# Finding a row's 32 top scores on the maxima of column quadruples, pairs and single columns, under a new instruction order

## Chip, cores and metric

The kernel runs on one core of a Trainium2 chip. The metric is the device time of one execution in microseconds (us). A core has TensorE (PE), VectorE (DVE), ScalarE (ACT), GpSimd (POOL) and SyncE (SP, which here only issues transfers); each works through its own list of instructions in program order, and semaphores tie the lists together.

## What is computed

Three parts follow each other: sparse attention, a mixture of experts with one expert per token, and a SoLU block. For the change only the first matters. There are 4 batches, 8 heads, 576 positions and head size 64.

```
scores = scale * np.matmul(q, k.transpose(0, 1, 3, 2))          # [4, 8, 576, 576]
kth  = np.partition(scores, -32, axis=-1)[..., -32:-31]          # the row's 32nd largest
scores = np.where(scores >= kth, scores, -1e9)
attn = softmax(scores);  x = attn @ v                            # 2304 tokens of 512
x = moe(x)      # gate, argmax expert e, relu(x @ w1[e]) @ w2[e], scaled by the gate
x = solu_block(x)   # x @ w_in, h * softmax(h), layer norm, @ w_out
```

So each of the 18432 rows of 576 scores needs its 32nd largest value as a threshold.

## The kernel before

**Units.** The attention is cut into 144 units: a tile of query rows against all 576 keys of one head (for the last 64 rows of a batch, of two heads). A unit's scores lie in two PSUM banks of 288 columns each, `pS[0]` and `pS[1]` (L628); one block of matmuls fills the banks of two units. There are 8 PSUM banks in all, and every other matmul group of the kernel uses them too.

**A unit's steps (function `unit`).** ACT copies both banks to `ss` in SBUF (L649, L659). DVE writes into `W` the larger of columns c and c+288 (`M`, L661) and the smaller (`m`, L662); then the two banks are given back. On the 288 values of `M` DVE takes the eight largest three times (L665, and L672 twice), and each time strikes them out with a match-and-replace (L669, which the profile shows as a short value load and the pass itself). A last pass takes the eight largest of what is left in all 576 columns of `W` (L678); its eighth is the row's threshold. POOL turns the threshold into a bias (L689), ACT and POOL mask the scores (L690, L691), ACT takes the exponential (L693). The largest value, negated and scaled on POOL (L666), is the bias of the exponential.

**Is the threshold right?** It is, as long as no more than eight of the row's top 32 are hidden behind a larger partner. `flags` in `route` checks this for a tile's units with three small POOL operations (L810 to L812): the threshold must not be above the eighth value of the third round, kept in `abt`. Where a row breaks it, the end of the kernel runs the whole attention again in another way; with the inputs here this part isn't entered.

**After the units.** `pair` transposes the weights of two units (L722), multiplies with v (L755) and projects (L765). `route` finds each token's expert and scatters its row to a list in DRAM. When enough tokens are routed (`PLAN`: the first slot at 256 tokens), a block of 128 tokens of one expert is gathered and goes through the two expert layers (L1025, L1046) and the SoLU block (L1067, L1128). The last expert work after the last unit has its own matmuls (L1326, L1346). Beside the first units, `doubles` and the `static_` functions turn the float64 weights `w_in` and `w_out` into pairs of float32 (DVE L386, L388, L390; POOL L385, L394; PE L408).

**Order.** All of this is written as generators. `Order.run` takes the next step from one of the threads that are ready, and which one is written out digit by digit in the string `ORDER`: it fixes the order of the instructions on every engine. The costs in `Op(...)` are not used when the string is given.

Of the kernel before, what the change touches and what calls it, by code (L numbers as in the profile page):

```python
# [8 lines left out]
F32 = mybir.dt.float32  # L9
# [5 lines left out]
OP = mybir.AluOpType  # L15
# [24 lines left out]
    "0022556001101111220112334441144455551445446666556657427747773222333327775335888447777436655355541288886662"  # L40
    "2233223377544545420880112434236636663555662111122220111115455512445515551511211444454422222112223333666113"
    "3677784664844663352111111114453311466771167444662422235434533444363637777333312222234322221144466551518833"
    "4435355339777288224444113324677688511211211155334446665565666222372233333113333445655777771161168722024833"
    "364422764382847945557586992411222555222a4488333989442aa292277444a33335563351353366887025343333211555467771"
    "8331873333226226676888853113114444112222551114666566788437777221214222352111138335117133335562222688137331"
    "1122666223222222235112441111112255451611114334444444133111111666656a147372244aa3a3677774455556119427135517"
    "7761261369999787111173632227776224251111133888171113445356658591113713163122241322220112222243111364111555"
    "5111156776334777754544116666657333522253254343442133244452226222233441611554545451145762678742523411524162"
    "22222225514322324455555555133155404551451162351344434336201166666773113222204472226565568117772222027a6644"
    "2266464472211535668637322022222226234211516656511613540701811001175772221192999991335336676626241121334343"  # L50
    "3422555576337144457752056556777776215277441122834266512111342551133443434111111321155111222312444312444689"
    "aa2333029166334862388066005582200012aaa0777bb8998934541622627600052200011131722264677550113332300005665771"
    "1170031302720170043355600466411520041444300222668822888899999882484113267676788595956678666666925441122656"
    "5651777834222574441772263345689181074232222220673604122673357761573325887774644455712263522222222664541341"
    "1045414324420011144552254555514660021440013400000024234556745440055522115552561878733155684688777751336544"
    "5522223362222205541140343146455552226111731022557441213374221168484911556614642265506443433375366777121111"
    "533706773363254599899a689548155555524459476611342216655611177671835511677634226577117786311153888645222222"
    "7771222233662545456605571436222443151232342444666511500012000440000313112111343433671170010055667322114331"
    "1363465555221111455220630073322228265511576466723111112603666353357006664700007700729944477777833a66688289"
    "0116a1119187115166734448376675373887777333833a122456647838833266776765567837833468512131331225837225554312"  # L60
    "8011202544504355355302277788226646344878976772222222331099482615452333043334466610030778151121467633320077"
    "7000003700555555666111661615657776300662449983332347756264545456668999a3033745564541133688784444699aa84781"
    "032284813361447676111114611868841110100915546644444488129878a77899896b7579467a8877122553999aaa892258444708"
    "45444333333126634452122553347773116433316611142222885344366112995522833b4477366622211544112322285673558511"
    "63633737112288887452220221166555562278855073355536111711460111aaa452289a88582123aabb498999aa40330330244496"
    "98a64001988a5511614744832110155578828474643998754087785533446633633226233620666666462231777177220776267884"
    "4348446940178787878666666789785261511884412377779974664537725512274646464677447367776122451172444562222213"
    "1225568816667421477776565657112322146554253325466222246225776345520223257717554223777754662253345563333342"
    "08227851115111066114456608000077777211265627589aa0155a9966185556667493355689994533444744444588337798996998"
    "9851155767678885588894411941545584422333663336222111153353114113354553652834547778223455456331677727777565"  # L70
    "6333332333365646666778722224111551122442551771134552423112222222373773354445892288777722222238444b37757527"
    "ab77771115325aa5888892472231118378838808794946466522988328482414663899988881121442997265651165651133344116"
    "25777777786746966a45579aaaabb744668747454442554918847833367676035669999777a1255115344931111222228868296353"
    "6456464664377311855255511552222122111534347766266115653678722465657752222544666256533011449352448433326467"
    "451573334457577162222533112266885272433689aa89956555222267679222788887393312242222131816766333478877775650"
    "254477757875753aa788328807553a91455826333388036733305422224263315653368888365557247333357722222599889634b3"
    "999222558789bb000755877333333888377088255558366a43333994660019a9a80733440000030444335664438744337766777000"
    "0042211138885555116166111333510000220511666221454444161157703633333464111166666576335782446651621173633625"
    "5053446016577644449359a50446757776133336643346637332783311557544440066650074330000436626667722774665543442"
    "2503433847777455277131111115662255346424336225643377205677116614589777888262222277163111006667334665755462"  # L80
    "2131747511070656565114444434455657000045566667777aabaa4111111b478879666bb754832244305365655779247227733530"
    "3333266477122335575030007577362545588944000566500688874ba7822210033613331566555452222200882233662652454544"
    "7577586657838504727671466726665664412273422522277667782644324228816711455244522656756587644566733221322444"
    "3338331666244422275500044006666200000564177552285333083304822222255136651100115656008057366660000446500077"
    "67700667a7724117703442320005357745664465566633333331151116753305354334555667772292960002224667776664211123"
    "22535355360725522223222244388377644473322815656556255227777721222264675239225772886888700a7782255611646565"
    "7916111118170036786443344735833838383004444441142551400641255124542004104023232322134444124544113112216671"
    "5277666524466956557347767762211117111116423325560355356772235744370111627666888247866224533355224833308858"
    "8223446441114555711111714432211443337750411442362152335407733300000666000055001334133331113444102334444122"
    "2200122200111111100112321122110000010000022334402022330000000001122222334422440304444331152234000333366666"  # L90
    "6666663333316334755001553444444435000551172233366222010204331133333302222220000111002222322322320033300246"
    "6611100011101103345522100222311131231112233443311102001000332222333002000000000001000000000000002330002223"
    "3222222330223314334443221143333221122452400220110000000000303011112210003301101111111111112222201110021120"
    "1111110302211110022110100000"
# [145 lines left out]
def attn_moe_solu_kernel(ctx, tc, q, k, v, mid, w_gate, mbias, w1, w2, w_in, w_out, g_ln, out):  # L240
# [49 lines left out]
    flag = cst.tile([128, H], F32, name="flag")  # L290
# [347 lines left out]
    def unit(b, t, p, s, abt, tht, u, no, done):  # L638
# [22 lines left out]
        tM = yield Op("DVE", 369, lambda: nc.vector.tensor_tensor(M, pS[1], ss[:, :HALF], op=OP.max), deps=[t0])  # L661
# [1008 lines left out]
```

## Time and profile before

| | us |
|---|---|
| three runs | 943.79, 941.67, 943.60 (median 943.6) |
| the profiled execution, its own time | 944.39 |
| span of the profiled execution, first to last instruction | 942.5 |
| busy: PE / DVE / ACT / POOL | 874.3 / 773.9 / 670.3 / 582.4 |
| mean granted TensorE clock, as a share of 2.4 GHz | 0.967 |

The time is that of the whole execution; the span inside it is 1.9 us shorter. Busy times are of engines that work side by side, so they don't add up to the span. A DVE instruction's duration reaches past the start of the next one: durations overlap, and what an instruction costs a full queue is the distance from its start to the next start.

### The profile page before, as it was taken

The page shows a single profiled execution, that of the slowest core. Times are in us where ns is not written, and L with a number is a line of the kernel's source. Part 1 is how long each engine was busy: PE and PEld are TensorE (multiplying, and loading weights), DVE is VectorE, ACT ScalarE, POOL GpSimd, SP SyncE. Part 2 cuts the span into 40 slices and gives each one's busy share as a digit, 9 for nine tenths or more (in the row PEclk, how much of TensorE's full clock was granted, in tenths as well). Part 3 has the DMA queues.
Part 4 walks back from the last instruction along what each step waited for, and adds up shares of the span by engine and source line. Part 5 has one row for each costly group of instructions (what it writes and reads, how often), then busy time and mean ns, then how long its engine had stood idle before and what let it go on. Part 6 is the DMA issues. An engine that isn't in the chain of part 4 may idle for free.

```text
span 942.5 us, 21521 instructions
## 1 busy us (share of the span) xinstructions
PE 874.3 (93%) x6830; PEld 729.7 (77%) x6830; DVE 773.9 (82%) x2444; ACT 670.3 (71%) x1698; POOL 582.4 (62%) x1352
## 2 busy tenths in 40 slices
PE   5876787999999999999999999999999999999994
PEld 3443445987888888888878888788888988889883
DVE  7899989998999999999999999999999952432331
ACT  4777776879787778888877898788778872633432
POOL 4677866667657676676476767766776676531223
PEclk9878788999999999999999999999999999999998
DMA  6624323534623343464334434443432337723001
GB/s 157 196 68 128 103 91 92 146 106 125 192 80 122 119 140 99 128 160 140 104 90 122 142 93 135 146 119 113 129 100 84 112 107 210 235 79 112 24 12 37
DMA packets 140952, 110.72 MB, mean 117 GB/s; under 512 B 47233, under 2 KB 116893, under 8 KB 140830
## 3 DMA queue, kind: packets, MB, share of 16 engines
q1 hardware_dynamic: 136478, 93.92, 34.8%
q0 software_dynamic: 4352, 15.34, 4.8%
q8 instruction: 56, 0.92, 0.4%
q14 instruction: 66, 0.54, 0.2%
HBM read 97.11 MB, written 12.13 MB: 116 GB/s over the span
## 4 chain that ended last, share of the span: by engine, by line
PE 64%; DVE 11%; POOL 6%; ACT 5%; issue 3%; DMA 1%; POOLq 0%; DVEq 0%; ACTq 0%
PE ph L1025 10%; PE ph L1067 9%; PE py L1046 9%; PE po L1128 8%; PE po L755 6%; PE pS L628 5%; PE pt L722 5%; DVE M L669 2%; PE py L1346 2%; PE ph L1326 2%; POOL e L691 2%; PE px L765 2%; PE pt L960 2%; PE pw L408 2%; DVE tht L678 1%
## 5 line engine op out<-in xcount | busy, mean ns | idle before, releaser
L691 POOL TENSOR_TENSOR e<-ss,e 128x576 f32<-128x576 f32 x144 | 204.7, 1423 | 55.6 <-ACT e L690 54.1
L693 ACT ACTIVATE e<-e,nb 128x576 f32<-128x576 f32 x144 | 111.8, 777 | 22.8 <-POOL e L691 22.1
L669 DVE MATCH_REPLACE8 M<-tops,M 128x288 f32<-128x288 f32 x288 | 127.6, 446 | 0.0
L1025 PE MATMUL ph<-xT,wraw 128*128 128x128 f32 x960 | 126.9, 279 | 0.0
L1046 PE MATMUL py<-hh,wraw 128*128 128x128 f32 x960 | 125.8, 278 | 0.0
L690 ACT ACTIVATE e<-ss,bt 128x576 f32<-128x576 f32 x144 | 111.1, 776 | 14.6 <-POOL bt L689 14.3
L1025 PEld LDWEIGHTS ph<-xT,wraw 128*128 128x128 f32 x960 | 115.5, 191 | 6.0 <-issue 3.8
L1046 PEld LDWEIGHTS py<-hh,wraw 128*128 128x128 f32 x960 | 115.4, 192 | 4.2 <-issue 2.4
L1128 PE MATMUL po<-wo,lT 128*128 128x512 f32 x432 | 112.3, 405 | 0.5 <-DVE lT L968 0.2
L755 PE MATMUL po<-eT,vt 128*64 128x128 f32 (+1 forms) x1600 | 105.1, 273 | 7.5 <-ACT eT L725 3.3
L1067 PE MATMUL ph<-wi,yT 128*128 128x512 f32 x432 | 109.7, 402 | 0.0
L678 DVE MAX8 tht<-M 128x8 f32<-128x576 f32 x144 | 108.0, 753 | 0.9
L755 PEld LDWEIGHTS po<-eT,vt 128*64 128x64 f32 x1600 | 85.0, 140 | 24.1 <-ACT eT L725 6.9
L628 PE MATMUL pS<-kT,qT 64*128 64x288 f32 (+1 forms) x864 | 91.5, 324 | 3.9 <-DVE M L662 2.8
L725 ACT ACTIVATE eT<-pt 128x512 f32<-128x512 f32 x144 | 82.4, 598 | 15.7 <-PE pt L722 14.9
L1128 PEld LDWEIGHTS po<-wo,lT 128*128 128x128 f32 x432 | 77.5, 188 | 20.7 <-DVE lT L968 3.4
L1067 PEld LDWEIGHTS ph<-wi,yT 128*128 128x128 f32 x432 | 78.5, 188 | 18.2 <-issue 1.2
L722 PE MATMUL pt<-identr,e 128*128 128x128 f32 x576 | 84.2, 280 | 6.2 <-ACT e L693 3.3
L628 PEld LDWEIGHTS pS<-kT,qT 64*128 64x128 f32 (+1 forms) x864 | 71.6, 197 | 20.7 <-issue 8.8
L722 PEld LDWEIGHTS pt<-identr,e 128*128 128x128 f32 x576 | 67.2, 144 | 15.5 <-ACT e L693 4.3
L649 ACT ACTIVATE ss<-pS 128x288 f32<-128x288 f32 x144 | 58.0, 411 | 22.1 <-PE pS L628 15.1
L661 DVE TENSOR_TENSOR M<-pS,ss 128x288 f32<-128x288 f32 x144 | 64.9, 451 | 9.9 <-ACT ss L659 7.7
(256 smaller groups left out, 1826.1 us busy)
## 6 DMA issues: line engine op xcount, KB each, us to landing
wraw<-in_moe_w_dram SPq DMA_DIRECT2D x256, 256.0 KB
kr<-in_k_dram SPq DMA_DIRECT2D x32, 128.0 KB
qr<-in_q_dram SPq DMA_DIRECT2D x16, 256.0 KB
raw<-in_moe_w_out_dram SPq DMA_DIRECT2D x8, 512.0 KB
vt<-in_v_dram SPq DMA_DIRECT2D x32, 128.0 KB
raw<-in_moe_w_in_dram SPq DMA_DIRECT2D x8, 512.0 KB
wstage<-da SPq DMA_DIRECT2D x8, 256.0 KB
wc<-wstage SPq DMA_DIRECT2D x8, 256.0 KB
```

Of the source, the lines that this page charges most:

```text
L628: nc.tensor.matmul(bank[s][hf], x[r, a, p, :], kt[r, c, at:at + HALF], start=i == 0, stop=i == 2)
L669: nc.vector.match_replace(out=M, in_to_replace=rounds[r], in_values=M, imm_value=NEG)
L678: t0 = yield Op("DVE", 660, lambda: nc.vector.max(th, W), deps=[t0, tm])
L690: yield Op("ACT", 667, lambda: nc.scalar.activation(e, ss, AF.Relu, bias=bt, scale=-BIG))
L691: yield Op("POOL", 1360, lambda: nc.gpsimd.tensor_tensor(e, ss, e, op=OP.subtract))
L693: yield Op("ACT", 760, lambda: nc.scalar.activation(e, e, AF.Exp, bias=nb, scale=0.125, accum_out=z))
L722: nc.tensor.transpose(pt[:, c, :], ef[:, at:at + 128], ident)
L755: nc.tensor.matmul(po[hs, :n], w, x, start=c == 0, stop=c == 4)
L1025: nc.tensor.matmul(ph[:, :n], w[:, kk * 128:(kk + 1) * 128], x[0][:, kk, :n], start=kk == 0, stop=kk == KD - 1)
L1046: nc.tensor.matmul(py[c // k_][:, c % k_, :], w[:, c * 128:(c + 1) * 128], hs[m], start=m == 0 and c % k_ == 0, stop=m == KF - 1 and c % k ...
L1067: nc.tensor.matmul(ph, y[a][:, kk, :], wi[b][:, kk, i * 512:(i + 1) * 512], start=kk == 0 and j == 0, stop=kk == KD - 1 and j == 2)
L1128: nc.tensor.matmul(po, l[a][:, c, :], wo[b][:, kk, :], start=kk == 0 and j == 0, stop=kk == KF - 1 and j == 2)
```

## The change

`W` is used in four quarters. `Q` is the largest of four columns (c, c+144, c+288, c+432), 144 values; it is built from two maxima of 144 (one of them written to the first half of the bank `pS[0]`) and their maximum, and their minimum goes to `q`, beside it. `m`, the smaller of each pair, is made as before. Two rounds of eight now run on `Q` (144 values), the third on `M` = `Q` and `q` (288), the last on all 576. The two banks are given back after the five elementwise operations instead of after two. `abt` holds nine values per unit, so that the eighth of the second round stands beside the eighth of the third, and `flags` compares the threshold with both: its three POOL operations are twice as wide. `ORDER` is replaced as a whole.

```
 ORDER = (
...
-    flag = cst.tile([128, H], F32, name="flag")
+    flag = cst.tile([128, 2 * H], F32, name="flag")
...
-        M, m = W[:, :HALF], W[:, HALF:]
+        M, m, Q, q = W[:, :HALF], W[:, HALF:], W[:, :HALF // 2], W[:, HALF // 2:HALF]
         th = tht[:, u]
-        tops = sb.tile([128, 16], F32, tag="tops", name="tops", bufs=BUF["tops"])
-        rounds = [tops[:, 0:8], tops[:, 8:16], abt[:, u]]
+        tops = sb.tile([128, 8], F32, tag="tops", name="tops", bufs=BUF["tops"])
+        rounds = [(tops, Q), (abt[:, u, 1:9], Q), (abt[:, u, 0:8], M)]
...
-        tM = yield Op("DVE", 369, lambda: nc.vector.tensor_tensor(M, pS[1], ss[:, :HALF], op=OP.max), deps=[t0])
+        h, g = HALF // 2, pS[0][:, :HALF // 2]
+        ta = yield Op("DVE", 215, lambda: nc.vector.tensor_tensor(Q, pS[1][:, :h], ss[:, :h], op=OP.max), deps=[t0])
+        tb = yield Op("DVE", 215, lambda: nc.vector.tensor_tensor(g, pS[1][:, h:], ss[:, h:HALF], op=OP.max), deps=[t0])
         tm = yield Op("DVE", 369, lambda: nc.vector.tensor_tensor(m, pS[1], ss[:, :HALF], op=OP.min), deps=[t0])
+        tq = yield Op("DVE", 215, lambda: nc.vector.tensor_tensor(q, g, Q, op=OP.min), deps=[ta, tb])
+        t0 = yield Op("DVE", 215, lambda: nc.vector.tensor_tensor(Q, g, Q, op=OP.max), deps=[ta, tb])
         yield "put", ("B", 2)
-        t0 = tM
-        t0 = yield Op("DVE", 369, lambda: nc.vector.max(rounds[0], M), deps=[t0])
-        tn = yield Op("POOL", 179, lambda: nc.gpsimd.tensor_scalar(nb, tops[:, 0:1], -0.125, None, op0=OP.mult), deps=[t0])
-        for r in range(3):
-            def mr(r=r):
-                nc.vector.match_replace(out=M, in_to_replace=rounds[r], in_values=M, imm_value=NEG)
-
-            def mx(r=r):
-                nc.vector.max(rounds[r + 1], M)
-
-            t0 = yield Op("DVE", 369, mr, deps=[t0])
-            if r < 2:
-                t0 = yield Op("DVE", 369, mx, deps=[t0])
+        for r, (best, among) in enumerate(rounds):
+            t0 = yield Op("DVE", 216 if r < 2 else 369, lambda: nc.vector.max(best, among), deps=[t0, tq])
+            if r == 0:
+                yield Op("POOL", 179, lambda: nc.gpsimd.tensor_scalar(nb, tops[:, 0:1], -0.125, None, op0=OP.mult), deps=[t0])
+            t0 = yield Op("DVE", 272 if r < 2 else 420, lambda: nc.vector.match_replace(
+                out=among, in_to_replace=best, in_values=among, imm_value=NEG), deps=[t0])
...
-            f = small("fl", H, F32, 2)
-            nc.gpsimd.tensor_tensor(f[:, :nu], tht[:, :nu, 7], abt[:, :nu, 7], op=OP.subtract)
-            nc.gpsimd.tensor_scalar(f[:, :nu], f[:, :nu], 0.0, None, op0=OP.is_gt)
-            nc.gpsimd.tensor_tensor(flag[:, :nu], flag[:, :nu], f[:, :nu], op=OP.add)
+            f = small("fl", 2 * H, F32, 2).rearrange("p (u r) -> p u r", r=2)[:, :nu]
+            sofar = flag.rearrange("p (u r) -> p u r", r=2)[:, :nu]
+            nc.gpsimd.tensor_tensor(f, bc(tht[:, :nu, 7], 2, 2), abt[:, :nu, 7:9], op=OP.subtract)
+            nc.gpsimd.tensor_scalar(f, f, 0.0, None, op0=OP.is_gt)
+            nc.gpsimd.tensor_tensor(sofar, sofar, f, op=OP.add)
...
-                abt = sb.tile([128, H, 8], F32, tag="ab", name="abt", bufs=BUF["xs"])
+                abt = sb.tile([128, H, 9], F32, tag="ab", name="abt", bufs=BUF["xs"])
```

## Rows read from the trace of the kernel before

**Rows 1.** The page's list of engines: busy us, share of the span, instructions.

```profile
PE 874.3 (93%) x6830; PEld 729.7 (77%) x6830; DVE 773.9 (82%) x2444; ACT 670.3 (71%) x1698; POOL 582.4 (62%) x1352
```

**Rows 2.** Busy time by stretch: stretch, its length, each engine, PEclk, DMA.

```profile
25.00:160.00 135.00, 102.44 (x565) 62.35 (x563) 124.90 (x341) 99.04 (x231) 95.97 (x142) 0.82 0.36 109
160.00:770.00 610.00, 599.52 (x5254) 520.46 (x5255) 579.33 (x1907) 491.34 (x1285) 412.50 (x1016) 0.99 0.42 122
770.00:905.00 135.00, 133.94 (x858) 119.36 (x855) 42.65 (x126) 56.40 (x136) 51.33 (x137) 1.00 0.40 122
905.00:943.00 38.00, 24.66 (x113) 19.22 (x111) 9.01 (x19) 13.06 (x24) 11.21 (x28) 0.88 0.08 30
```

**Rows 3.** PE in order of time within 260 to 300 us.

```profile
275.85 1.95 PE L1046 MATMUL py<-hh,wraw 128*128 128x128 f32 x16
277.73 1.31 PE L755 MATMUL po<-eT,vt 128*64 128x128 f32 x20
```

**Rows 4.** L678 alone by stretch, as before (one per unit).

```profile
0.00:25.00 25.00, 1.42 (x2) 1.00 0.64 164
25.00:160.00 135.00, 15.05 (x20) 0.82 0.36 109
160.00:770.00 610.00, 91.52 (x122) 0.99 0.42 122
```

**Rows 5.** DVE's groups by line and shape: busy us, mean ns, idle before.

```profile
L669 DVE MATCH_REPLACE8 M<-tops,M 128x288 f32<-128x288 f32 x288 | 127.6, 446 | 0.0
L678 DVE MAX8 tht<-M 128x8 f32<-128x576 f32 x144 | 108.0, 753 | 0.9
L665 DVE MAX8 tops<-M 128x8 f32<-128x288 f32 x144 | 65.2, 453 | 0.0
L661 DVE TENSOR_TENSOR M<-pS,ss 128x288 f32<-128x288 f32 x144 | 64.9, 451 | 9.9 <-ACT ss L659 7.7
...
L669 DVE MATCH_VALUE_LOAD M<-tops,M 128x8 f32 x288 | 23.5, 82 | 0.7
...
L776 DVE TENSOR_TENSOR xs<-px,rz 128x144 f32<-128x144 f32 x16 | 4.8, 299 | 0.0
```

**Rows 6.** DVE in order of time, 305 to 310 us: start, duration, instruction.

```profile
305.75 0.45 DVE L662 TENSOR_TENSOR M<-pS,ss 128x288 f32<-128x288 f32 x1
306.12 0.45 DVE L665 MAX8 tops<-M 128x8 f32<-128x288 f32 x1
306.48 0.07 DVE L669 MATCH_VALUE_LOAD M<-tops,M 128x8 f32 x1
306.54 0.44 DVE L669 MATCH_REPLACE8 M<-tops,M 128x288 f32<-128x288 f32 x1
306.90 0.08 DVE L669 MATCH_VALUE_LOAD M<-tops,M 128x8 f32 x1
...
307.69 0.29 DVE L776 TENSOR_TENSOR xs<-px,rz 128x144 f32<-128x144 f32 x1
307.90 0.08 DVE L669 MATCH_VALUE_LOAD M<-abt,M 128x8 f32 x1
...
308.69 0.75 DVE L678 MAX8 tht<-M 128x8 f32<-128x576 f32 x1
309.35 0.08 DVE L669 MATCH_VALUE_LOAD M<-tops,M 128x8 f32 x1
```

**Rows 7.** DVE in order of time, 12 to 14 us, with few units in flight.

```profile
12.89 0.45 DVE L672 MAX8 tops<-M 128x8 f32<-128x288 f32 x1
13.37 0.09 DVE L669 MATCH_VALUE_LOAD M<-tops,M 128x8 f32 x1
```

**Rows 8.** PE's longest wait of 160 to 770 us: us, times, longest.

```profile
PE px L765 <- ACT e L690: 4.6, 1, 4.6
```

**Rows 9.** What PE waited for over the whole span, one row.

```profile
PE pS L628 <- DVE M L662: 2.8, 2, 2.6
```

**Rows 10.** POOL's flag operation at two widths.

```profile
L811 POOL TENSOR_SCALAR fl<-fl 128x8 f32<-128x8 f32 x16 | 4.2, 264 | 1.4
...
L811 POOL TENSOR_SCALAR fl<-fl 128x4 f32<-128x4 f32 x4 | 1.0, 250 | 0.4
```

More of the change, by code (lines that the diff above doesn't have):

```diff
@@ L45 @@
[L45 to L59, printed above, removed]
@@ L90 @@
[L90 to L94, printed above, removed]
+    "0025526001101111220233225455555554444644111414433664354511112666666011133373577483888838446666666245555660"
@@ new lines @@
+    "4002111033300118511718884332255343434443334000011113351115523264446655515177114177557712363445270350500644"
+    "4433522232155215555526205550114466266634601111446444336552443331336555333111114475522666633665563633366511"
+    "7777777222233222226554421622244466556771447777777112221337644141172264455322226666665602012240001113222222"
+    "220005545111345446544554667660076832255656667887117116a222393826440555554617222433448376798228188441188878"
+    "2221513333361337222215504440044337744554220000066626433226466505451545454461666661113230412126551116004455"
@@ new lines @@
+    "6666656001115003443635500555405400441155511154444000222222223455000366001111667644211111881111877030222234"
+    "0404040001434000100302444443001155556003344777a226000aaa557a8677712267777733002289999931411101113250066666"
+    "5444244430000855888873511325011111144111523224631356663336614222721116551114503440002288888555855350450036"
+    "3551631322453344443435111444442263111114554436120223000302323232444444131135617811100672227055055522245555"
+    "1100335355353142424252055555000007777444011440076867767772255311115511812222226355887777888992447770122407"
@@ new lines @@
+    "3627142226773533333330644555225231454545111441116666611611670440001416622522224777777772666600033344444431"
+    "1154226151111343427756660167898676125733311557766634771644666352221615561111134343424322661114113112789677"
+    "4937339328522778799935c5998aa9aa00000001888c6c445797989891811337888888254425302000011141113333761714415300"
+    "5550011023360008112223520043366611152444530100333113177115001177777788888887394567864411564485555557674655"
+    "2552111156224545454466557766666848466756aaa8661441778966759988ab21ba777797a3d36698333399888883403753318867"
@@ new lines @@
+    "2312333343566511656613226611544422330444445466115544555220666454000000004132323440055613364655555501178337"
+    "7737557711788546377774431558345554522584557111345531111100466622225535105161122757315333574435112511112607"
+    "776773111100006646447733123222542247777476776333765776618045588999999988b641592444223335334433775521544555"
+    "6666611165144331166577787676711723233777777356116652222222243316612524548866563255545564546343224555545475"
+    "1777323255111314226745770440500030043224343534448981120000001889432711112555554555511112222011177835563441"
@@ new lines @@
+    "113434634555703111577767757922a96057008338897771715511166688811889544312011189781189991aa58844313444588167"
+    "6767776733377772228222655355887776677889978787338787999948284784683368881611157772222211222175264645521466"
+    "6668988869a44a633435a5455330222221455445475471226666336611344050666001100350005522224552117111155555557777"
+    "770033114464665111514693887174967744286280347575664466656669996766999aa4177665333316745444ab55821715a55569"
+    "885758778722266778222892299999778922299119b677272676433264868777776316656533906478676157777773949937854344"
@@ new lines @@
+    "4366561443330223352367741437447776722524225333329664425556299315775577333726aa6452222237766626155574733394"
+    "63355756378887878111129844245011176621188522728845578542224757222288551166aaaaa1118471ab53889966299aa86918"
+    "881199299995555111466722004433228111254aa22121344400554544105160114434454611166336411111511577777777388888"
+    "887846633115334034677999440c518989899336666777886618898888866133222288833557331223232557757757885766565652"
+    "33525267566661777462222711222253366881245646536699a2699816515446345555415455244622666331115627216676011733"
@@ new lines @@
+    "11234434343562101432556255863615551112222622778311665111154166048111467799999b244699557a3377a396bb0a7a7a77"
+    "8a1193aa4666979964894333445aaaaaa5444645774338589899817986871153188668788888422961117761176884441151334492"
+    "2322662226663329370407537766767644775888888123471344430455445666665052277777152226022457700554346000514444"
+    "4021034655031101111112044343430503400455334556667891773443811111144715555577226440177122637478787711119771"
+    "1116688878722299aa99333118a9999211533888886a3cc9979744911719797991124669aa19999993417332287781714432882878"
@@ new lines @@
+    "77535882478777222288226a785b42662988a99aaaaa722288a221b746677299772789422222334533223825757575557988884448"
+    "8666330444611224422666651114145658866563114524630aa7533655333533366666667945411356539974493333248586553336"
+    "752222577466656111122335622279a9975bb885133770232030042255117623550105504905500676622778833315656557778888"
+    "896948666895999929222224a465477884301558776739a99898aaaaaaa14444444776566224443766107770004664111111771144"
+    "55777299222388888899999622222225887a800a348700455268885833664500a4459aaaa811451053600470770033333000635604"
@@ L95 @@
+    "4411466111001222000003345522222043324422201111522550262501133001233321111111221020000000000000002200000000"
+    "0000001111111111122211212222211133220111244212213333222122003111130000021133311110011111331110020020222331"
+    "110223000101111200022111110000000000"
 )
```

50 lines of the change are left out of this document (15 added, 35 removed).

## The prediction, made before the change was run

> **What bounds the kernel now.** Read the engines' shares first [rows 1]: PE 874.3 us of 942.5, DVE 773.9. The averages don't say which of them sets the time; the stretches do [rows 2]. From 160 to 770 us PE is busy 599.5 of 610 us and from 770 to 905 us 133.9 of 135, at a granted clock of 0.99 and 1.00 of 2.4 GHz. That it is really full there, and not waiting inside long matmul records, is seen in its order of time [rows 3]: sixteen L1046 run from 275.85 and the next group starts at 277.73, 1.88 us later, with no gap. DVE looks nearly full there too, 579.3 of 610. But units end by 770 us, and 135 us of pure PE work follow, in which DVE is busy for 42.7: expert blocks that had piled up behind PE. If the units end earlier, those blocks are still there, and PE has as much left to do.
>
> Before 160 us it is otherwise. From 25 to 160 us PE is busy 102.4 of 135 us at a clock of 0.82, and DVE 124.9. No expert block can start before 256 tokens are routed, so here the units set the pace, with the preparation of the SoLU weights beside them on DVE, POOL and PE. A microsecond taken out of this stretch comes off the end, because everything behind it is a full PE. The last 38 us hold PE for 24.7 and no unit; the change doesn't touch them.
>
> How many units lie in front? L678 runs once per unit: 2 plus 20 start before 160 us, 122 after [rows 4].
>
> **The elementwise steps and rounds on DVE.** First the price of an instruction. Its duration includes a tail in which the next one already runs: L665 starts at 306.12, the value load at 306.48, the replace at 306.54, the next load at 306.90, each while its predecessor is still recorded [rows 6]. So in a full queue a pass over 288 values costs 0.365 us (0.36 and 0.37 in these rows), the load 0.06, L678's 576 values 0.66. The difference of 0.30 us for 288 values is 1.04 ns per value, so a pass over 144 should cost 0.365 - 0.150 = 0.215. One row has such a pass: L776, two operands, one of them in PSUM, 144 values, 307.69 to 307.90, 0.21 us.
>
> Before, per unit: two elementwise passes 0.730, three maxima 1.095, three loads and replaces 3 x 0.425 = 1.275, the last 0.66; sum 3.76. After: four passes of 144 and one of 288, 0.860 + 0.365 = 1.225; maxima 0.215 x 2 + 0.365 = 0.795; replaces 0.275 x 2 + 0.425 = 0.975; the last 0.66; sum 3.655. The change saves 0.105 us a unit, 15.1 us of DVE over 144 units. The shorter rounds save 0.60 a unit and the three further elementwise passes give 0.495 of it back.
>
> Of the new passes one writes PSUM and two read what it wrote. No DVE instruction of before writes PSUM, so its price is bounded: below by L776's 0.21, above by what L661 costs at double the width, 0.365, as if halving had brought nothing. At the upper end three passes cost 0.15 more each, and the unit comes to 3.655 + 0.45 = 4.105, 0.345 more than before. I take the lower: reading PSUM costs nothing that shows (L661 451 ns with PSUM, L665 453 without [rows 5]), and L776 is the same operation at the same width.
>
> **What of it reaches the end.** The 22 early units save 22 x 0.105 = 2.3 us in the stretch that they pace. The 122 others save 12.8 us on an engine that runs beside a full PE. What they can still give is PE's own idle time, 610 - 599.5 = 10.5 us. Its longest wait is on a masked score, which comes off L678 by way of POOL and ACT (4.6 us, once [rows 8]); one quarter of the 10.5, 2.6 us, is my choice for what a less crowded DVE returns. Bounds: none of it, and all of it.
>
> **The banks.** A unit's two PSUM banks now wait for five passes: from the first start to the last end 4 x 0.215 + 0.365 + 0.09 of tail = 1.32 us, where it was 0.365 + 0.45 = 0.82. That is 0.5 us more. PE's next score block waited for this release 2.8 us in all, twice [rows 9]. In the same proportion (1.32 / 0.82) it becomes 4.5, 1.7 more, at most; I cost it at nothing, because each order can put other PE groups into so short a hold, and keep 1.7 as its upper end.
>
> **POOL and the rest.** Eight values against four cost 14 ns more in the flags [rows 10]; 8 more in each of three operations of 20 tiles are 60 x 0.028 = 1.7 us of POOL, which is busy 412.5 of 610 us and is hidden by that. Nothing waits for a flag until the end of the kernel. No transfer is added or moved past another by the steps themselves. L666 still follows the first round, which starts 3 x 0.215 - 0.15 = 0.5 us later in the unit, and isn't needed until the exponential, long after.
>
> **The order.** It decides every gap, and no row prices it. It can gain at most what PE loses in front: 32.6 us idle from 25 to 160 us, and a clock of 0.82 in its 102.4 busy us, worth 18.4 at full clock. It can lose as easily. I take zero for it, with some 6 us to either side in the range.
>
> Sum on the profiled execution: 944.4 - 2.3 - 2.6 = 939.5 us. The median of the three runs lies 0.8 below that execution, so the forecast is 938.7 us.
>
> **Rivals.** *Each pass waits for the one before it (slower).* With few units in flight the tail isn't hidden: after the maximum at 12.89 the load that needs it starts at 13.37, 0.48 instead of 0.365 [rows 7]. The new unit has 12 passes where there were 9, more of them dependent on the pass just before. By full durations [rows 5] before costs 2 x 451 + 3 x 453 + 3 x 528 + 753 = 4598 ns, after 4 x 299 + 450 + 2 x 303 + 453 + 2 x 378 + 528 + 753 = 4742, 144 ns more. It decides from about one further unhidden wait per unit on (0.115 against 0.105 saved). All 144 units would bring DVE 20.7 us; the 22 early ones put 3.2 on the time, and of the other 17.6, which meet 30.7 us of idle DVE, perhaps a third: 944.4 + 3.2 + 5.9 = 953.5, or 952.7 on the median's scale; with the early ones alone 946.8. Against it: from 305 to 310 us the neighbours are passes of other units, and the overlap is there each time. The Trainium skill, "VectorE: DVE Perf Modes", The DRAIN you can't avoid, says as much as this rival in general: the next operation does not start until the pipe is empty, so that one should minimise the count of operations. By that rule the change adds time; the trace disagrees in a full queue, where 0.45 us passes start 0.36 apart, and agrees for the dependent pair at 12.89.
>
> *PSUM written by DVE is dear (slower).* At the upper bound above: 22 x 0.345 = 7.6 in front, and 122 x 0.345 = 42 against 30.7 of idle, 11 over: 963.
>
> *DVE was the bound after all (faster).* All 15.1 us come off: 929.3, 928.5 on the median's scale. For it: DVE is busy 95% of 160 to 770. Against it: the backlog behind 770 us. An order that fills the front better ends in the same place.
>
> *Nothing reaches the end (same).* The early units were paced by POOL and PE's weight preparation as much as by DVE, and the order's small losses cancel the rest: 941 to 946.
>
> **Chances.** Forecast (a few us off, 935 to 941) 0.42; DVE or a better front (928 to 935) 0.14; nothing (941 to 946.5) 0.25; waits (946.5 to 953) 0.14; dear PSUM (to 963) 0.05. Runs of this kernel can tell some 0.3%, 2.8 us, from no change: faster is below 940.8. That takes the second case and 0.38 of the first, 0.52; slower is above 946.4, 0.19 and a little of the third, 0.20; the same 0.28. The range is 930 to 950: it leaves out some 0.02 below, and above it the dear PSUM and about half of the waits, 0.12. The likeliest case alone is 935 to 941.
>
> **What would show it.** Right: elementwise passes of 144 near 300 ns, maxima near 303, replaces near 296, starts 0.21 apart; DVE's sum down by some 15 us by starts, though its durations add up to more; PE's total busy time unchanged at full clock, the units' end before 770 us, a longer pure PE stretch behind it, and the whole gain in front of some 160 us. Wrong: PE idle from 160 to 770 us grows beyond 10.5 (banks, waits); the pass that writes PSUM takes near 450 ns; or PE's clock and idle time in front move by more than 5 us, in which case the order and not the arithmetic set the time.

## Result and the profile after

| | kernel before | changed kernel |
|---|---|---|
| median of nine runs each | 943.49 us (940.26 to 945.19) | 948.59 us (945.51 to 950.72) |
| ratio, with its 95% interval | 1 | 1.0054 [1.0039, 1.0069] |
| profiled execution, its own time | 944.39 us | 945.71 us |
| span; mean granted TensorE clock | 942.5 us; 0.967 | 943.9 us; 0.965 |

The change costs 5.1 us where 4.9 us of gain were forecast. The time lies inside the range given, on the other side of no change. The profiled execution of the changed kernel is the second fastest of its nine: its rows can account for 1.4 us, not for the whole 5.1.

First the page's list of engines, which answers to [rows 1]:

```profile
PE 873.2 (93%) x6830; PEld 731.8 (78%) x6830; DVE 769.9 (82%) x2876; ACT 671.6 (71%) x1698; POOL 581.7 (62%) x1352
```

PE does the same work in 1.1 us less. DVE issues 432 instructions more, three per unit, and its busy time, in which passes that overlap count once, is 4 us less. Then the stretches, which answer to [rows 2], with one further cut at 180 us. The first row is the kernel before in that cut, the others are the changed kernel:

```profile
160.00:180.00 20.00, 19.12 (x168) 17.63 (x169) 19.37 (x63) 15.35 (x41) 11.32 (x24) 0.85 0.54 151
...
25.00:160.00 135.00, 100.02 (x557) 61.33 (x557) 118.59 (x383) 96.91 (x224) 92.83 (x129) 0.82 0.35 104
160.00:180.00 20.00, 14.14 (x102) 11.98 (x103) 19.47 (x76) 12.74 (x32) 13.30 (x30) 0.74 0.37 118
160.00:770.00 610.00, 598.73 (x5252) 522.17 (x5253) 581.14 (x2284) 494.16 (x1291) 415.57 (x1026) 0.99 0.42 123
770.00:905.00 135.00, 133.39 (x856) 119.09 (x855) 42.54 (x127) 55.00 (x135) 50.36 (x136) 1.00 0.41 124
```

From 25 to 160 us PE is idle for 35.0 us instead of 32.6. From 160 to 180 us it is busy for 14.14 us at a granted clock of 0.74; the kernel before had 19.12 at 0.85 there. In the rest, 180 to 770 us, its idle time is 11.27 - 5.86 = 5.4 us, where it was 10.48 - 0.88 = 9.6. So for PE the changed kernel is 2.4 + 5.0 us worse from 25 to 180 us and 4.2 us better from there to 770. The front is late: the first gather of an expert's tokens (L935) starts at 165.8 us, 159.7 before (L933 there). The last units' last passes start 1.4 us later, at 768.3 (766.9 before). Before, then after:

```profile
L933 POOL DMA_INDIRECT xg<-xlist,li x14: 1079/1090/1133, 159.7 to 778.7; - x14
...
L935 POOL DMA_INDIRECT xg<-xlist,li x14: 1069/1092/1126, 165.8 to 780.1; - x14
L679 DVE MAX8 tht<-M x144: 731/751/762, 19.9 to 768.3; 128x8 f32<-128x576 f32 x144
```

What did the new passes cost? DVE by line and shape (busy us, mean ns, idle before), which answers to [rows 5]. L666 and L667 are the two halves of the first maximum (L667 writes PSUM), L668 the minimum of the pairs, L669 and L670 the minimum and the maximum of the halves, L673 the rounds, L676 the replaces, L679 the last pass:

```profile
L679 DVE MAX8 tht<-M 128x8 f32<-128x576 f32 x144 | 107.7, 750 | 1.0
...
L668 DVE TENSOR_TENSOR M<-pS,ss 128x288 f32<-128x288 f32 x144 | 64.4, 447 | 0.0
...
L667 DVE TENSOR_TENSOR pS<-pS,ss 128x144 f32<-128x144 f32 x144 | 43.9, 305 | 0.2
L670 DVE TENSOR_TENSOR M<-pS,M 128x144 f32<-128x144 f32 x144 | 43.9, 305 | 3.8 <-issue 0.2
L666 DVE TENSOR_TENSOR M<-pS,ss 128x144 f32<-128x144 f32 x144 | 43.0, 299 | 10.5 <-ACT ss L663 8.6
L669 DVE TENSOR_TENSOR M<-pS,M 128x144 f32<-128x144 f32 x144 | 42.8, 297 | 0.0
...
L673 DVE MAX8 tops<-M 128x8 f32<-128x144 f32 x144 | 42.5, 299 | 0.7
L676 DVE MATCH_REPLACE8 M<-tops,M 128x144 f32<-128x144 f32 x144 | 42.0, 292 | 0.0
```

Every pass has the duration that was forecast or nearly so, the one into PSUM too (305 ns). What the durations don't show are the distances from start to start. DVE in order of time (start, duration), two places of the same kernel:

```profile
265.99 0.30 DVE L669 TENSOR_TENSOR M<-pS,M 128x144 f32<-128x144 f32 x1
266.32 0.31 DVE L670 TENSOR_TENSOR M<-pS,M 128x144 f32<-128x144 f32 x1
266.55 0.30 DVE L666 TENSOR_TENSOR M<-pS,ss 128x144 f32<-128x144 f32 x1
266.76 0.31 DVE L667 TENSOR_TENSOR pS<-pS,ss 128x144 f32<-128x144 f32 x1
...
284.78 0.30 DVE L669 TENSOR_TENSOR M<-pS,M 128x144 f32<-128x144 f32 x1
284.99 0.08 DVE L676 MATCH_VALUE_LOAD M<-abt,M 128x8 f32 x1
285.06 0.29 DVE L676 MATCH_REPLACE8 M<-abt,M 128x144 f32<-128x144 f32 x1
285.27 0.30 DVE L670 TENSOR_TENSOR M<-pS,M 128x144 f32<-128x144 f32 x1
```

L666 to L667 is 0.21 us, a pass of 144 at its price. L669 to L670 at 265.99 is 0.33, and L670 starts only when L669's recorded 0.30 us are over. Where other work stands between them (284.99, 285.06) nothing waits. L670 doesn't read what L669 wrote. It overwrites `Q`, which L669 reads. I took each instruction's usual distance to the next start as its price and counted, in the DVE's order from 160 to 770 us, the gaps of 0.07 to 0.16 us beyond it: some 225 of them, 26 us in all, against some 95 and 11 us before (the counts move by a few per cent with what is taken as usual). 87 of the 225 stand in front of L670, some 47 in front of a round L673. Without such gaps DVE's occupied time there fell by some 7 to 8 us, with one unit more in the stretch (123 for 122); some 15 us went into new gaps.

Last the waits of PE up to 200 us (total, times, longest), which answer to [rows 9]:

```profile
PE pw L412 <- DVE da L392: 5.4, 3, 2.7
...
PE pS L632 <- DVE M L668: 3.9, 3, 1.7
PE pt L723 <- DVE kT L537: 3.6, 1, 3.6
```

The score matmuls (L632) wait for DVE's use of the banks for 3.9 us, three times, and no more than that over the whole span; it was 2.8, twice. The pass that ends these waits, L668, is the last reader of `pS[1]`, not of `pS[0]`.

### The profile page after: what moved, and what is told of

Its sections match the earlier page's. It is cut to its first block, busy times and chain, and to the rows that moved or that the text cites. A ratio compares the mean times of both kernels' runs of the same rounds, so it can differ in the third digit from the quotient of the medians.

```text
span 943.9 us, 21968 instructions
## 1 busy us (share of the span) xinstructions
PE 873.2 (93%) x6830; PEld 731.8 (78%) x6830; DVE 769.9 (82%) x2876; ACT 671.6 (71%) x1698; POOL 581.7 (62%) x1352
## 4 chain that ended last, share of the span: by engine, by line
PE 70%; DVE 11%; POOL 7%; ACT 5%; issue 3%; DMA 3%; SPq 0%; POOLq 0%; DVEq 0%; ACTq 0%
PE ph L1027 10%; PE py L1048 10%; PE ph L1069 9%; PE po L1130 8%; PE po L756 8%; PE pS L632 7%; PE pt L723 5%; PE pw L412 3%; PE ph L1328 2%; PE py L1348 2%; PE px L766 2%; PE pt L962 2%; DVE M L676 2%; POOL e L692 1%; DVE tht L679 1%
## 5 line engine op out<-in xcount | busy, mean ns | idle before, releaser
L679 DVE MAX8 tht<-M 128x8 f32<-128x576 f32 x144 | 107.7, 750 | 1.0
L756 PE MATMUL po<-eT,vt 128*64 128x128 f32 (+1 forms) x1600 | 102.4, 272 | 5.4 <-ACT eT L741 1.9
L673 DVE MAX8 abt<-M 128x8 f32<-128x288 f32 (+1 forms) x288 | 104.8, 375 | 1.7
L676 DVE MATCH_REPLACE8 M<-abt,M 128x288 f32<-128x288 f32 (+1 forms) x288 | 105.2, 367 | 0.0
L632 PE MATMUL pS<-kT,qT 64*128 64x288 f32 (+1 forms) x864 | 92.9, 320 | 10.4 <-DVE M L668 3.9
L723 PE MATMUL pt<-identr,e 128*128 128x128 f32 x576 | 86.3, 286 | 10.2 <-DVE kT L537 3.6
L632 PEld LDWEIGHTS pS<-kT,qT 64*128 64x128 f32 (+1 forms) x864 | 71.6, 192 | 27.5 <-issue 7.0
L723 PEld LDWEIGHTS pt<-identr,e 128*128 128x128 f32 x576 | 69.1, 147 | 20.1 <-issue 5.2
```

What stands on the lines that cost most here:

```text
L632: nc.tensor.matmul(bank[s][hf], x[r, a, p, :], kt[r, c, at:at + HALF], start=i == 0, stop=i == 2)
L676: t0 = yield Op("DVE", 272 if r < 2 else 420, lambda: nc.vector.match_replace(out=among, in_to_replace=best, in_values=among, imm_value=NE ...
L679: t0 = yield Op("DVE", 660, lambda: nc.vector.max(th, W), deps=[t0, tm])
L723: nc.tensor.transpose(pt[:, c, :], ef[:, at:at + 128], ident)
L756: nc.tensor.matmul(po[hs, :n], w, x, start=c == 0, stop=c == 4)
```

## Experiments

All have five rounds, and each ratio is to the kernel before, timed on the same chip. Three explanations stood open at first: the order, the dependent neighbours on DVE, and the hold on the banks.

**Steps and order apart.** The change replaces a unit's steps and the whole order. *e1* keeps the new steps and replays the old order (its slot for the first pass goes to L666 and L667, its slot for the second to L668, L669 and L670). *e2* is the kernel before in the new order, with empty steps in the three slots that it has no pass for:

```
         tM = yield Op("DVE", 369, ... max), deps=[t0])
+        yield Op("DVE", 0, lambda: None, deps=[t0])
         tm = yield Op("DVE", 369, ... min), deps=[t0])
+        for _ in range(2):
+            yield Op("DVE", 0, lambda: None, deps=[t0])
```

> The unit's new passes (quadruples, pairs, all) under the order of the kernel before: every step of every engine where it stood, the first two new passes in the place of the old maximum, the next three in the place of the old minimum. Theory O (the new order's front costs the time, the new passes save a little): the forecast's sum, 2 to 5 us below the kernel before, ratio 0.995 to 0.998, first gather again near 160 us. Theory W (the new passes cost time in any order, through waits on each other or the longer hold of the PSUM banks): ratio 1.003 to 1.007, first gather some 3 us or more later than before.

> The old passes under the new order (the old maximum where the new kernel starts its five passes, the old minimum where it has its own, nothing in the places of the other three). Theory O: still slower than the kernel before, and by at least as much as the changed kernel, ratio 1.005 to 1.010, first gather 5 us or more late. Theory W: no slower than before, ratio 0.998 to 1.002.

Measured: e1 1012.04 us, 1.0732 [1.0709, 1.0755]; e2 945.26 us, 1.0023 [1.0013, 1.0034]. The new order with the old steps costs 2.2 us, and the new steps in it 3 more. In e2 the loss is in front, 3.0 us less PE work from 25 to 160 us and 1.8 less from 160 to 180:

```profile
25.00:160.00 135.00, 99.41 (x563) 61.43 (x562) 125.69 (x338) 97.50 (x228) 94.25 (x135) 0.87 0.35 105
160.00:180.00 20.00, 17.36 (x138) 14.89 (x138) 19.76 (x64) 14.28 (x38) 12.35 (x26) 0.74 0.52 153
```

But in the old order the new steps cost 69 us: the order cannot be blamed and left at that, because the steps cannot live without it. In e1 the units end at 835.9 us, and PE's wait for the banks is 7.2 us in eight pieces:

```profile
PE pS L632 <- DVE M L668: 7.2, 8, 2.2
...
L679 DVE MAX8 tht<-M x144: 733/749/764, 21.7 to 835.9; 128x8 f32<-128x576 f32 x144
```

**Front and rest apart.** Both with the new steps: *e3* has the old order up to the first expert slot and the new one from there, *e4* the reverse. Only `ORDER` differs.

> The new passes; the old order up to the first step of the first expert slot (about 160 us), the new order for all that is left. Theory O: the time of the first run of this call or better, since the new order's later part lost nothing in the traces (ratio 0.994 to 0.998). If the loss lies in the new order behind the front: 1.003 to 1.006. Theory W: 1.003 to 1.007.

> The reverse: the new passes, the new order up to the first step of the first expert slot, the old order for all that is left. Theory O: slow, like the changed kernel, ratio 1.003 to 1.008, first gather near 166 us. If the loss lies behind the front: 0.995 to 0.999. Theory W: 1.003 to 1.007, so this run tells O from W only together with the others.

Measured: e3 964.01 us, 1.0223 [1.0197, 1.0249]; e4 997.40 us, 1.0589 [1.0562, 1.0617]. Wherever the old order is used with the new steps it loses: 21 us with it in front, where some 22 of the 144 units lie, and 55 us with it behind. No single place breaks it.

**The dependent neighbours.** *e5* keeps the new order and takes the overwriting away: the first pass writes a spare tile in SBUF, the maximum of the halves goes first, and the minimum beside it no longer meets it. Four units, in which the spare tile would be needed twice at once, keep the old way.

```
+        A = Q if no in TIGHT else spare
-        ta = ... tensor_tensor(Q, pS[1][:, :h], ss[:, :h], op=OP.max)
+        ta = ... tensor_tensor(A, pS[1][:, :h], ss[:, :h], op=OP.max)
-        tq = ... tensor_tensor(q, g, Q, op=OP.min)
-        t0 = ... tensor_tensor(Q, g, Q, op=OP.max)
+        for op in ((OP.min, OP.max) if no in TIGHT else (OP.max, OP.min)):
+            t0 = ... tensor_tensor(Q if op == OP.max else q, g, A, op=op)
```

> The changed kernel under its own order, with the first pass of a unit written to a spare tile of 144 columns instead of into Q, and the pass that makes Q put ahead of the one that makes q (4 units keep the old way). The last of the five passes then overwrites nothing that its neighbour reads, and the first maximum has a pass between it and the one that it needs. The banks are held as long as in the changed kernel. Theory D (passes that wait for the pass right before them eat the saving: about 100 of 144 units lose 0.12 us at the fifth pass): DVE loses some 12 us of waits, the time falls 2 to 6 us below the changed kernel, ratio to the kernel before 0.998 to 1.003. Theory H (the longer hold of the banks): unchanged, 1.004 to 1.007. Theory O (the order alone): unchanged too.

Measured: 944.60 us, 1.0011 [0.9998, 1.0023], so 4.0 us less than the change as made, with intervals that don't meet. Its passes have the same durations, and DVE's busy time from 160 to 770 us is 6.2 us less. Counted as above, some 100 of the 225 gaps and 11 us of them are gone; 87 of these are the ones in front of L670, most of the rest stood between L670 and the round that reads its result.

```profile
L672 DVE TENSOR_TENSOR M<-pS,spare 128x144 f32<-128x144 f32 x280 | 74.8, 297 | 0.0
...
160.00:770.00 610.00, 599.38 (x5271) 523.17 (x5272) 574.90 (x2288) 493.26 (x1292) 416.62 (x1028) 0.99 0.42 123
```

*e10* has the same passes in the old order (one unit keeps the old way).

> The same passes with the spare tile under the order of the kernel before (the first run of the last call, which took 1012 us, with the neighbouring dependent passes taken apart; 1 unit keeps the old way). Theory D: most of its 69 us come back, 940 to 960. Theory H: it stays above 1000, because the banks are held as long. Theory O (an order fits only the steps that it was made for): it stays above 990.

Measured: 1007.79 us, 1.0690 [1.0666, 1.0715]. The neighbours are not what breaks the old order; some 4 of the 69 us go, with intervals that just overlap.

**What DVE time is worth.** *e8* is the kernel before with a shorter last pass; it leaves out 101 columns of each row:

```
-        t0 = yield Op("DVE", 660, lambda: nc.vector.max(th, W), deps=[t0, tm])
+        t0 = yield Op("DVE", 660, lambda: nc.vector.max(th, W[:, :475]), deps=[t0, tm])
```

> The kernel before with its order, but the last pass of each unit looks at 475 of the 576 columns (it leaves out 101): the forecast's 0.105 us per unit taken off DVE and nothing else changed, no bank held longer, no pass added. The forecast's step (2.3 us in front, 2.6 behind): ratio 0.993 to 0.998. Theory P (PE is full and the front is paced by other things, so what DVE saves doesn't arrive): 0.999 to 1.001.

Measured: 940.54 us, 0.9973 [0.9962, 0.9984]: 2.5 us for a pass that takes 644 ns instead of 753, some 15.6 us in all.

```profile
L678 DVE MAX8 tht<-M 128x8 f32<-128x475 f32 x144 | 92.4, 644 | 0.9
...
160.00:770.00 610.00, 601.38 (x5288) 522.34 (x5287) 566.81 (x1903) 492.68 (x1289) 413.13 (x1020) 1.00 0.42 121
```

Its first gather starts 2.1 us earlier (157.5) and DVE is busy 12.5 us less from 160 to 770 us, while PE's busy time there rises by 1.9, of which 0.9 lies before 180. The profiled executions are 3.7 us apart, more than the medians.

**The banks.** *e6* keeps the new order and steps but writes the second half's maximum to the spare tile instead of into `pS[0]`, which frees that bank early:

```
-        h, g = HALF // 2, pS[0][:, :HALF // 2]
+        h, g = HALF // 2, pS[0][:, :HALF // 2] if no in TIGHT else spare
```

> The changed kernel under its own order, with the second maximum of 144 written to the spare tile in SBUF instead of into the first bank (4 units keep the old way): the first bank is free after ACT's copy and the second after the third pass, as before the change, while the passes wait for each other as in the changed kernel. Theory H: 2 to 5 us below the changed kernel, ratio 0.999 to 1.003. Theory D or O: unchanged, 1.004 to 1.007.

Measured: 984.12 us, 1.0440 [1.0422, 1.0458]. It doesn't answer its question, because the passes with both inputs in SBUF became slow. By line and shape, then min/median/max of one line:

```profile
L671 DVE TENSOR_TENSOR M<-spare,M 128x144 f32<-128x144 f32 x140 | 71.6, 511 | 3.4
L670 DVE TENSOR_TENSOR M<-spare,M 128x144 f32<-128x144 f32 x140 | 68.9, 492 | 0.0
...
L671 DVE TENSOR_TENSOR M<-spare,M x140: 278/309/1605, 11.3 to 800.1; 128x144 f32<-128x144 f32 x140
L671 DVE TENSOR_TENSOR M<-pS,M x4: 307/307/308, 60.4 to 564.5; 128x144 f32<-128x144 f32 x4
```

*e9* asks it from the other side. It is the kernel before, in its own order, with one pass reading the same values from their other copies, so that `pS[0]` is held until DVE's second pass and not only until ACT's copy:

```
-        tm = ... tensor_tensor(m, pS[1], ss[:, :HALF], op=OP.min)
+        tm = ... tensor_tensor(m, pS[0], ss[:, HALF:], op=OP.min)
```

*e11* takes the hold away from e10, in the old order: the minimum goes first, the second half's maximum overwrites `pS[1]`, which is done with by then, and `pS[0]` is free after ACT's copy. (One unit keeps the old destination of the first pass.)

```
-        h, g = HALF // 2, pS[0][:, :HALF // 2]
+        h, g = HALF // 2, pS[1][:, HALF // 2:]
...
+        tm = ... (m, pS[1], ss[:, :HALF], min)
+        ta = ... (A, pS[1][:, :h], ss[:, :h], max)
+        tb = ... (g, pS[1][:, h:], ss[:, h:HALF], max)
+        maximum of g and A into Q, minimum into q
```

> The kernel before with its order; the minimum reads the first bank and the second half of the copy, where it read the second bank and the first half: the same values, and the first bank is held until DVE's second pass instead of ACT's copy. Theory H (the hold of the first bank is what breaks the old order under the new steps): slower by 10 us or more, ratio over 1.01. Theory N (the first maximum comes later and POOL's queue stands behind the step that waits for it) and theory O: 0.999 to 1.002.

> The old order with the new steps and the spare tile, as in the run that took 1008 us, but the minimum first and the second maximum written over the second bank, so that the first bank is free after ACT's copy. Theory H: under 980. Theory N and O: 1000 to 1015 (one dependent pair stands together, some 0.12 us a unit).

Measured: e9 996.04 us, 1.0580 [1.0553, 1.0607]; e11 953.52 us, 1.0114 [1.0091, 1.0137]. The one line that holds `pS[0]` longer costs the kernel before 54 us. Taking the hold away gives back 54 of e10's 65 us. In e9 PE's wait for the banks and DVE's wait for ACT's copy, and the stretch from 160 to 770 us:

```profile
PE pS L628 <- DVE M L661: 11.3, 6, 5.3
...
DVE M L661 <- ACT ss L659: 24.3, 24, 5.0
...
160.00:770.00 610.00, 578.67 (x4935) 495.44 (x4934) 554.09 (x1814) 462.83 (x1208) 392.94 (x973) 0.98 0.40 116
```

The waits in e9 end with L661, which reads `pS[1]`; none of PE's matmuls waits for L662, the pass that holds `pS[0]`. So PE is seen waiting for the bank of the pair that DVE frees first, and no longer has the one that ACT's copy used to free. Which bank a later matmul group is given is settled when the program is built, and as built e9 hands them out in another order than the kernel before; no run separates that from the hold itself.

In e11 that wait is small again (there the release is by L672, the maximum and minimum of the halves):

```profile
PE pS L633 <- DVE M L672: 1.4, 1, 1.4
```

*e14* has e11's passes in the new order, four units the old way.

> The new order with the spare tile, the minimum first and the second maximum written over the second bank, so that the first bank is free after ACT's copy (4 units keep the old way); tb and tQ, a dependent pair, now stand together in some 116 units, as tq and tQ did in the changed kernel. If the hold still costs time under the order that was made with it: below the changed kernel by 2 us or more, 1.000 to 1.003. If that order has worked around the hold, and only the waits are left: 1.003 to 1.007.

Measured: 947.70 us, 1.0061 [1.0042, 1.0080], the same as the change as made. But in e14 the second half's maximum (L670) often stands right before the maximum that needs it (L672), and often right behind the other half's (L669), which reads the bank that it overwrites. Over the whole span 118 such L672 start 0.35 us after L670 and 105 L670 start 0.33 us after L669, where 0.21 is usual: 16 and 12 us of waits, against 12 us between L669 and L670 in the change as made. So e14 has more waits and the same time. The free bank may well pay for the difference; the two effects are not separated there.

**POOL's queue.** *e12* (from e10) and *e13* (from e5) issue the exponential's bias `nb`, which waits for the first round, only next to `bt`, so that nothing queues behind it on POOL:

```
-                yield Op("POOL", 179, ... tensor_scalar(nb, tops[:, 0:1], -0.125, ...), deps=[t0])
+                yield Op("POOL", 0, lambda: None, deps=[t0])
...
+        yield Op("POOL", 358, ... bt and nb together), deps=[t0])
```

> The old order with the new steps and the spare tile, as in the run that took 1008 us, but POOL's small step on the first maximum (the bias of the exponential) is issued next to the one on the threshold, so that POOL's queue no longer waits for the first maximum. Theory N: most of the 65 us come back, 945 to 970. Theory H and O: 995 to 1010.

> The same late bias under the new order with the spare tile (the run at ratio 1.0011). The new order was made for the new steps, so POOL should wait little for the first maximum there: theory N 0.998 to 1.001, theory H and O 0.999 to 1.003. If it comes below 0.9985 it is the best version with the new steps.

Measured: e12 1003.59 us, 1.0654 [1.0626, 1.0683], 4 us better than e10 with intervals that overlap; e13 948.27 us, 1.0059 [1.0037, 1.0080], 4 us worse than e5. This queue is at most a small term in the old order, and moving the bias doesn't help in the new one.

**The rest of e11.** *e15* is e11 with another unit's DVE step pulled between the second half's maximum and the maximum that needs it, in 124 units (order alone, and four units the old way).

> The old order and the new steps with the first bank free, as in the run that took 953.5 us, and in 124 units one DVE step of another unit pulled in between the dependent pair. If the dependent pair (0.12 us of DVE a unit) makes most of the 11 us that are left: 942 to 947, ratio 1.000 to 1.005. If it is the longer hold of the second bank or the later first maximum: 950 to 956.

Measured: 963.90 us, 1.0229 [1.0208, 1.0250], 10 us worse than e11. The pulls took away 16 of the 19 us of waits between L670 and L672, but new waits in front of other passes gave 6 of them back, and the kernel still lost 10 us, so the moved steps cost more than was left. e15 also leaves e11's other pair as it was: L670 starts 0.33 us after L669 in some 90 units of both, 11 us of DVE. What the last 11 us of e11 are stays open: the longer hold of the second bank, the later first round and the two pairs were not told apart.

## Why the prediction was wrong

A gain of 4.9 us was forecast, and the change costs 5.1. Three terms of the sum failed: the saving on DVE, of which waits between neighbours took most; the new order, at zero; and the banks, at nothing, whose share under the new order is not shown.

**Right.** The arithmetic of the passes: 292 to 305 ns for every pass of 144, PSUM no dearer, so the lower price was the right end. POOL's wider flags left no mark (its busy time is 581.7 us, 582.4 before). And DVE is not the bound: 15.6 us less of it, taken from the last pass in e8, gave 2.5 us. That the time lies inside the stated range says little: the range left 6 us to either side for an order that no row priced.

**The saving was mis-sized by half.** The forecast was 2.3 us in front and 2.6 behind 160 us, 4.9 together. e8 removes as much, in the same units, and gives 2.5. Its first gather moves 2.1 us, near the 2.3. That would leave some 0.4 for the term "one quarter of the 10.5, 2.6 us", which was a choice and not a reading; but PE's busy time behind 160 us rises too, so which of the two terms is short is not shown. With the new order the same saving, without the neighbours, is e2 to e5: 945.26 to 944.60 as times, 1.2 thousandths as ratios, some 1.1 us with intervals that overlap.

**First failed step: "The banks", at nothing.** It said that both banks had been held for DVE's two passes and now were held for five, 0.82 to 1.32 us, and costed that at nothing, at most 1.7 us. The first half was false. In the kernel before both DVE passes read `pS[1]` and the copy of `pS[0]` in `ss`; `pS[0]` itself was done with when ACT's copy L649 ended. The kernel before has a wait of PE's weight group that ends with L649, which I had not followed up:

```profile
PE pw L408 <- ACT ss L649: 3.1, 1, 3.1
```

Writing the intermediate maximum into `pS[0]` holds it until the last elementwise pass. In the old order taking this hold on or off is 54 us, as e9 and e11 show from both sides, 30 times my upper end. It shows little as waits on the score matmuls, 11.3 us in e9 where it was 2.8. The likely way, not followed step by step, is that every engine takes its list in order: a late bank delays the ACT copy, the DVE passes behind it (24.3 us where it was 7.7) and each later step of other units that stands behind those. What the hold costs in the change as made, under the new order, is not shown (e14).

**Second failed step: "The order", at zero.** An order that has the units wait for five passes had to be another one, and it is 2.2 us worse even for the old steps (e2). The price lies in front: 4.8 us less PE work from 25 to 180 us in e2. As the old order suits the new steps badly, part of the 2.2 may be that the new order suits the old ones less; that is not separated. I had treated order and steps as independent, with chances of either sign; they are not. That the new order was arranged so because of the hold is argued from e1 and e14, not shown.

**Third failed step: the saving on DVE, in which no pass waited for its neighbour.** That was left to the rival "each pass waits", at a chance of 0.14. Its mechanism is the largest loss that the runs show in the change as made: 4.0 us to e5. Its window, 946.5 to 953 us, holds the 948.6, partly by luck, since 2.2 of the loss are the order's. Its argument against, that neighbours in a full queue are passes of other units, held for the kernel before and not for the new order. The new order puts L669 and L670 side by side in 104 of the 144 units. And I looked only for passes that need a result; here the second overwrites an input of the first, which costs the same 0.12 us. 104 x 0.12 = 12.5 us takes most of the 15.1 saved. Some third of the lost DVE time reached the end, 4.0 us of the some 11 that e5 took away from 160 to 770 us, as the rival had guessed.

**The account.** By ratios to before: 1.0000, then 1.0023 with the new order (e2), 1.0011 with the new steps without the neighbours' waits (e5), 1.0054 with them. That is +2.2 - 1.1 + 4.1 = 5.2 us. As each term is the step from one run to the next, they must come to the 5.1 measured, but for rounding; the sum is no proof, and another path (by e1: +69, then -64) splits it otherwise. The terms come from runs on different chips, each against before on its own, and the middle one is not clear of zero. Against the forecast, the saving is 1.1 us where it was 4.9, and 2.2 and 4.1 stand where nothing stood. No kernel here that computes the same was faster than before; e5 equals it within its interval.

## What to carry to other kernels

Before a bank or tile is reused as scratch, find which engine's last access frees it now, and count how much later the new last access is; here, under an order made for the early release, the delay came back many times over. Neighbours on DVE waited for each other here when the second overwrites an input of the first as well as when it reads its output, so give the result another place or put one other step between. Where steps and a written-out order change together, time all four combinations before either is credited or blamed.

## What the runs showed of the hardware

An overwriting neighbour starts 0.33 us after a pass of 144, an unrelated one 0.21 us after it. In the trace the overwriting L670 has a wait on the semaphore that DVE's own instructions count up, so the program makes it wait. The Trainium skill, "VectorE: DVE Perf Modes", The DRAIN you can't avoid, says that the next operation does not start until the pipe is empty, and that one that isn't held starts earlier; the trace agrees with the first for the dependent pair (0.33 us, when the 0.30 of the pass before are over) and with the second for unrelated neighbours (0.21).

A DVE pass on two tensors in SBUF took up to 1.605 us in e6, against 0.308 at most with one of them in PSUM, and POOL's pass L693 over `ss` and `e` takes 1.437 us. The mean of L671 in e6 is 511 ns, that of the same pass in the change as made 305. Of the 280 passes with both inputs in SBUF 69 took over 0.35 us. 58 of these overlap an L693 in time, though L693 is busy for only 206 of the 982 us, and each of the other 11 overlaps another POOL instruction. The Trainium skill, "SBUF — State Buffer", Who interferes with whom, says that a DVE instruction with two SBUF inputs contends with a GpSimd instruction that reads SBUF, and that one of the two then blocks; e6 agrees in the overlap and in the size of the longest passes, though no run here varied POOL's work by itself. With the intermediate in PSUM the change as made avoids this, and holds the bank longer instead.
